# A larger landing allowance for streamed weight halves and parked value rows in a hand-planned two-layer transformer kernel

## The chip, the cores and the metric

The kernel runs on one core of one Trainium2 chip. The metric is the device time of one execution in microseconds. The kernel before takes 3228.07 us, the median of three executions (3224.22 to 3236.77 us).

## What is computed

Two layers stand one after the other twice: A, an attention with a recurrent memory, and B, a mixer and an MLP. The sequence has 2048 rows of width 640 in bf16. A works on 64 segments of 32 rows; 8 memory rows come ahead of each segment, and the first 8 rows of a segment's output are the memory of the next one, so the segments follow one another strictly. It has 32 heads of width 192.

```python
def _A_ref(x, mem0, Wq, Wk, Wv, Wo, seg_len):
    mem = mem0
    for s in range(n_seg):                      # 64 segments
        h = concat([mem, x[:, s*32:(s+1)*32, :]], axis=1)      # 40 rows x 640
        q, k, v = h @ Wq, h @ Wk, h @ Wv        # 32 heads x 192
        p = softmax(where(mask, q @ k.T * scale, -1e9))
        o = (p @ v) @ Wo
        mem = o[:, :8, :]; outs.append(o[:, 8:, :])

def _B_ref(x, w1, w2, w3, w4):
    h = gelu(layernorm(x) @ w1)
    hs = shifted_quarters(h) @ w2               # rows shifted by 1 and 2, both ways
    x1 = x + hs
    return x1 + gelu(layernorm(x1) @ w3) @ w4   # 640 -> 1536 -> 640

x = x + A(layernorm(x)); x = x + B(layernorm(x))
x = x + A(layernorm(x)); x = x + B(layernorm(x))
```

## The kernel before

**Steps and lanes.** The two passes through A run in one loop of 69 steps. In step t lane 0 does segment t of the first A and lane 1 segment t-5 of the second A (`LAG = 5`), so that steps 5 to 63 have both lanes, with 80 rows together, and the five steps at either end have one lane with 40. The B layers run beside it in chunks of 64 rows per lane, one chunk for two steps (`chunk`, `chunk_end`).

**One step.** The 32 heads are 8 groups of four, taken as four pairs. For a group TensorE makes keys and queries (`keys_queries`, L1789, tiles psk and psq, 30 matmuls of 80 columns for each), then scores (L1914, tile pss), the transposed probabilities (L1949, pst), the weighted values (L1966, pso) and the output projection (L1992, psy). Values of a pair are made at once: in an odd step for the two steps t and t+1 together (L1836), the rows of the next step being parked in DRAM (`vahead`, stored at L1844 by the POOL queue) and fetched back in the even step (L1874), in which TensorE makes only the 32 rows that were missing (L1863). The B chunk puts its matmuls (L2299, L2359, L2422, L2468) between these.

**Weights.** Wq, Wk and Wv do not all fit into SBUF. Of the five blocks of 128 input rows, `STREAM` gives for each pair how many are streamed in every step (4, 2, 2, 4 for keys and queries, 3, 1, 1, 4 for values); the others stay resident (tiles wk, wq, wv). A streamed block of a pair comes as two halves, one for each group, 128 x 768 bf16 or 192 KB each (`load_pair`, L1647, tile wst). They go into a ring of 24 slots (`RING_A`). The order of pairs is reversed in odd steps, so that the last pair of a step is the first of the next one and its halves, 22 or 24 slots, stay in the ring over the step's end. B's weights come in tiles of up to 320 KB (`load_b`, L1683 to L1689, tile wstB) through three slots. All of these loads are issued by the SP queue.

**The plan.** The program is first written as a list of operations, each with an engine, a duration, what it reads and writes, and the bytes of its DMA if it is one. `Plan.add` gives each a priority from the table `RANK`: one number for each operation of a kind of step (all even steps with both lanes share "step0", all odd ones "step1", the chunks between the ends "chunk" and "chunk_end"), in units of 1/67108864 us counted from the step's nominal start at 48 us a step. `Plan.place` sorts the operations of every engine by that number, and this sorted line is the order in which the engine's instructions are issued. It then walks through all lines with the durations and finds a planned start and end for each operation. A transfer is planned so:

```python
srv = max(s + DMA_FIRST, srv) + o.dma / (DMA_START if o.due < STEP else RATE_ONE if alone(o) else DMA_RATE)
done = srv + DMA_LAST + o.margin
```

with `DMA_FIRST = 0.8`, `DMA_LAST = 3.2` and `DMA_RATE = 315.0e3` bytes a microsecond. `done` is when the plan lets readers start. Three things follow from the planned times. The slots of a ring (and the PSUM banks) are given to operations in the order in which the plan sees them come free. A load that the plan holds back so as not to run ahead of the transfers in flight is marked `paced`, and is made to wait for the last TensorE operation that the plan has finished by then (`PACE`, at the end of the program). And the list in which instructions are written out is the plan's. The engines themselves know nothing of planned times: they run their line in order and wait for semaphores.

Loads of half blocks had no margin, B's loads have 0.6 us (`B_MARGIN`), the two `vahead` transfers had 0.7.

**Around a step's end.** The memory columns of the next step are copied from psy by VectorE (L2019). The rows of the next segment of lane 1 come from the chunk two steps before: transposes on TensorE (L2522, `ft4`) and copies into hT by ScalarE (L2530, `fc`). The first keys of a step read both.

Of the kernel before, what the change touches and what calls it, by code (L numbers as in the profile page):

```python
# [29 lines left out]
LOOK = 48  # L30
# [26 lines left out]
DMA_ISSUE = 0.37  # L57
# [21 lines left out]
        "apply_ln.f": (619821940, 1419652867, 3136865741, 3492529800,),  # L79
        "chunk.f1": (-1862542,),  # L80
        "chunk.f2": (535234527,),
        "chunk.f3": (1353287692,),
        "chunk.fe": (870238683,),
        "chunk.fe3": (3486582945,),
        "chunk.fel": (1557734022,),
        "chunk.fhr": (1765481928,),
        "chunk.fhs": (3007050626,),
        "chunk.fk0": (326638728,),
        "chunk.fk1": (2726001406,),
        "chunk.fs": (3218780102, 3249069099,),  # L90
        "chunk.ft": (240166152,),
        "chunk.ftl": (1496228237,),
        "chunk.fw": (1622229593, 1701935762, 1679143945, 3102708780, 2859414961, 2758250835, 3572172952,
            3606843237, 3536726401, 4173573343, 4121567882, 4086897597, 4513907470,),
        "chunk.fx": (280917415,),
        "chunk.fx0": (1611157029, 1591751692,),
        "chunk.fxu": (3495585980,),
# [6 lines left out]
        "load_b.fn": (-375525581, -730077448, -719610040, 2385923537, 2300994965, 2236236914, 2786142732,  # L104
            2909490384, 3152783868, 3707910948, 3558408627, 3606655073, 4125914395,),
        "transposes.f": (692464316, 3455587541,),
    },
    "chunk_0": {
        "apply_ln.f": (232141763, 341066263, 2067097874,),
        "chunk.f1": (-8505083173,),  # L110
        "chunk.f2": (-3934198857,),
        "chunk.f3": (429532210,),
        "chunk.fe": (489648082,),
        "chunk.fe3": (2067500527,),
        "chunk.fel": (489756973,),
        "chunk.fhr": (890745413,),
        "chunk.fhs": (1309035218,),
        "chunk.fk0": (947777863,),
        "chunk.fs": (1483668581, 1483869908,),
        "chunk.ft": (8946517,),  # L120
        "chunk.ftl": (632649931,),
        "chunk.fw": (771015019, 772787850, 771440545, 1256902217, 1257159630, 1256986807, 2238393962,
            2223390616, 2230674554, 2933112234, 2722326263, 2721658280, 3302745147,),
        "chunk.fx": (48195564,),
        "chunk.fx0": (732303114, 704855262,),
        "chunk.fxu": (2308563139,),
# [6 lines left out]
        "load_b.fn": (-3381292124, -3550034551, -865167426, 661737317, 901566278, 877089128, 1887363173,  # L133
            1723063724, 1770985122, 2367901289, 1963995011, 1996230009, 2750184683,),
        "transposes.f": (232343089, 1986629510,),
    },
    "chunk_1": {
        "apply_ln.f": (234352147, 424171623, 1139471209, 2036067845,),
        "chunk.f1": (-2741551,),
        "chunk.f2": (234150821,),  # L140
        "chunk.f3": (615954977,),
        "chunk.fe": (846136918,),
        "chunk.fe3": (2142881513,),
        "chunk.fel": (1047394441,),
        "chunk.fhr": (1126500078,),
        "chunk.fhs": (1691122064,),
        "chunk.fk0": (629977546,),
        "chunk.fk1": (783871166,),
        "chunk.fs": (1764784013, 1837791043,),
        "chunk.ft": (37634002,),  # L150
        "chunk.ftl": (679799131,),
        "chunk.fw": (1069660796, 1087512398, 1069363349, 1633744337, 1639274557, 1638655619, 2164198979,
            2250875979, 2143082840, 2698140225, 2881958716, 2728577128, 3229969347,),
        "chunk.fx": (77677747,),
        "chunk.fx0": (1019473581, 982935782,),
        "chunk.fxu": (2162451645,),
# [6 lines left out]
        "load_b.fn": (-579470846, -623813017, -964754743, 1067636933, 1158283287, 1183355579, 1764991342,  # L163
            1842237442, 1752739776, 2259173599, 2382650117, 2334628335, 2800447638,),
        "transposes.f": (399648704, 2036269172,),
    },
    "chunk_2": {
        "apply_ln.f": (292538731, 581557556, 1720999575, 2087329837,),
        "chunk.f1": (-1067306343,),
        "chunk.f2": (-917191276,),  # L170
        "chunk.f3": (383995904,),
        "chunk.fe": (571492627,),
        "chunk.fe3": (2206858353,),
        "chunk.fel": (574304103,),
        "chunk.fhr": (1075922126,),
        "chunk.fhs": (1728010341,),
        "chunk.fk0": (142581676,),
        "chunk.fk1": (1048460664,),
        "chunk.fs": (1730498649, 1730699975,),
        "chunk.ft": (6693347,),  # L180
        "chunk.ftl": (454388984,),
        "chunk.fw": (795548396, 873443794, 964470025, 1661674941, 1712556472, 1730190881, 2417607530,
            2407364944, 2408544805, 2859361305, 3144040297, 2867698681, 3424642378,),
        "chunk.fx": (21942750,),
        "chunk.fx0": (454590310, 464307541,),
        "chunk.fxu": (2124830409,),
# [6 lines left out]
        "load_b.fn": (-1455669518, -1022821962, -1141274702, 977129502, 914535287, 1285206154, 1774812963,  # L193
            1813367340, 1806473275, 2519856677, 2545492615, 2511697104, 2589146350,),
        "transposes.f": (292740058, 2192345064,),
    },
    "chunk_end": {
        "apply_ln.f": (6207473151,),
        "chunk_end.fc": (6407041413, 6407041413, 6932872812,),
        "chunk_end.fs": (5783564718, 5813267330,),  # L200
        "chunk_end.fst": (6203127175, 6017353691,),
        "chunk_end.ft4": (6406840087,),
        "chunk_end.fw": (5008812969, 5667704631, 5308788779, 5110805706, 5701443477, 5735182323,),
        "chunk_loads.f": (6259009269, 5903203514, 6038126415, 6070862680, 6014976291,),
        "ln_ops.f1": (5842969942,),
        "ln_ops.f2": (6164006683,),
# [1209 lines left out]
def kernel(  # L1416
# [17 lines left out]
    P = 128  # L1434
# [10 lines left out]
    GW = HG * Dh  # L1445
# [8 lines left out]
    VP = 2 * Dh + 64  # L1454
# [130 lines left out]
    add = plan.add  # L1585
# [1047 lines left out]
```

## Time and profile before

| What | Before |
|---|---|
| median of three executions | 3228.07 us (3224.22 to 3236.77) |
| the profiled execution, its own time | 3227.25 us |
| span of the profile, first to last instruction | 3225.5 us |
| mean granted TensorE clock | 0.991 |
| TensorE matmul busy | 3106.5 us |
| TensorE weight load busy | 2765.5 us |
| VectorE, ScalarE, GpSimd busy | 2052.9, 1723.4, 497.3 us |
| moved by DMA | 859.75 MB, mean 267 GB/s |

The profiled execution lies within the three others, so its times can be set beside their median. What remains between its time and its span, 1.75 us, lies outside the instructions. PE stands for TensorE's matmuls, PEld for its weight loads, DVE for VectorE, ACT for ScalarE, POOL for GpSimd, SP for the queue that issues the weight loads. An entry "X <- Y" in a list of waits says that engine X sat idle until Y released it.

### The profile page before, as it was taken

The page shows a single profiled execution, that of the slowest core. Times are in us where ns is not written, and L with a number is a line of the kernel's source. Part 1 is how long each engine was busy: PE and PEld are TensorE (multiplying, and loading weights), DVE is VectorE, ACT ScalarE, POOL GpSimd, SP SyncE. Part 2 cuts the span into 40 slices and gives each one's busy share as a digit, 9 for nine tenths or more (in the row PEclk, how much of TensorE's full clock was granted, in tenths as well). Part 3 has the DMA queues.
Part 4 walks back from the last instruction along what each step waited for, and adds up shares of the span by engine and source line. Part 5 has one row for each costly group of instructions (what it writes and reads, how often), then busy time and mean ns, then how long its engine had stood idle before and what let it go on. Part 6 is the DMA issues. An engine that isn't in the chain of part 4 may idle for free.

```text
span 3225.5 us, 161658 instructions
## 1 busy us (share of the span) xinstructions
PE 3106.5 (96%) x70199; PEld 2765.5 (86%) x70201; DVE 2052.9 (64%) x6448; ACT 1723.4 (53%) x3985; POOL 497.3 (15%) x983
## 2 busy tenths in 40 slices
PE   5889999999999999999999999999999999999898
PEld 4778889988888888888889888888888888888776
DVE  2565666666666666666666666666666666666665
ACT  1334555555555555555555555555555555556443
POOL 0001111111111111111111111111111111110000
PEclk7999999999999999999999999999999999999999
DMA  9887888888888888888888888888888888888786
GB/s 362 264 279 246 255 282 267 258 259 271 265 263 267 277 252 255 263 283 260 260 277 272 258 256 266 276 263 260 280 263 257 258 269 269 263 263 284 245 281 213
DMA packets 636978, 859.75 MB, mean 267 GB/s; under 512 B 72254, under 2 KB 622863, under 8 KB 636264
## 3 DMA queue, kind: packets, MB, share of 16 engines
q1 hardware_dynamic: 612056, 796.18, 77.5%
q0 software_dynamic: 24032, 53.12, 5.4%
q8 instruction: 550, 9.01, 1.2%
q14 instruction: 164, 1.34, 0.1%
q10 hardware_dynamic: 176, 0.09, 0.0%
HBM read 823.73 MB, written 25.37 MB: 263 GB/s over the span
## 4 chain that ended last, share of the span: by engine, by line
PE 80%; DMA 14%; issue 2%; DVE 1%; ACT 1%; POOL 0%; SPq 0%; POOLq 0%; ACTq 0%; DVEq 0%
PE psy L1992 16%; PE psk L1789 15%; PE psq L1789 15%; PE psv L1836 11%; DMA wst<-in_A_Wk_dram 6%; PE pso L1966 4%; PE pss L1914 4%; DMA wst<-in_A_Wq_dram 4%; PE psh L2422 3%; PE psv L1863 3%; PE y L2468 3%; PE pst L1949 2%; PE hs L2359 1%; PE psv L1894 1%; DMA wst<-in_A_Wv_dram 1%
## 5 line engine op out<-in xcount | busy, mean ns | idle before, releaser
L1789 PEld LDWEIGHTS <-wst 128*128 128x128 bf16 x19872 | 822.0, 99 | 127.8 <-DMA wst<-in_A_Wk_dram 31.7
L1992 PE MATMUL psy<-oT,wo 128*128 128x80 bf16 (+1 forms) x16560 | 695.9, 200 | 3.2 <-issue 1.0
L1992 PEld LDWEIGHTS <-wo 128*128 128x128 bf16 x16560 | 628.8, 99 | 27.6 <-issue 13.8
L1789 PE MATMUL psk<-hT,wst 128*128 128x80 bf16 (+1 forms) x9936 | 568.1, 200 | 37.2 <-DMA wst<-in_A_Wk_dram 23.3
L1824 ACT CAST V<-psv 128x384 bf16<-128x384 f32 (+4 forms) x1032 | 485.8, 474 | 199.1 <-PE psv L1863 75.5
L1789 PE MATMUL psq<-hT,wst 128*128 128x80 bf16 (+1 forms) x9936 | 550.0, 200 | 26.0 <-DMA wst<-in_A_Wq_dram 21.3
L1799 ACT CAST qT<-psq 128x480 bf16<-128x480 f32 (+1 forms) x552 | 291.5, 528 | 519.3 <-PE psq L1789 441.7
L1814 DVE CAST kT<-psk 64x160 bf16<-64x160 f32 (+1 forms) x1104 | 339.2, 307 | 132.6 <-PE psk L1789 87.8
L1937 DVE TENSOR_REDUCE sm<-Pm 80x4 f32<-80x320 bf16 (+2 forms) x552 | 249.9, 453 | 248.1 <-ACT Pm L1933 243.2
L1974 ACT CAST oT<-pso 128x480 bf16<-128x480 f32 (+1 forms) x552 | 293.8, 533 | 164.1 <-PE pso L1966 147.8
L1926 DVE CUSTOM_DVE_ANT_1 pss<-pss,mask 80x320 f32<-80x320 f32 (+2 forms) x552 | 258.0, 468 | 186.6 <-PE pss L1914 112.5
L1933 ACT ACTIVATE Pm<-pss,sm 80x320 bf16<-80x320 f32 (+2 forms) x552 | 279.7, 507 | 170.6 <-DVE sm L1926 107.7
L1957 ACT COPY PT<-pst 80x320 bf16<-80x320 bf16 (+2 forms) x552 | 221.3, 401 | 203.4 <-PE pst L1949 182.8
L1789 PE MATMUL psk<-hT,wk 128*128 128x80 bf16 (+1 forms) x6624 | 320.7, 200 | 2.0 <-issue 1.3
L1789 PE MATMUL psq<-hT,wq 128*128 128x80 bf16 (+1 forms) x6624 | 320.0, 200 | 2.5 <-DMA wq<-in_A_Wq_dram 1.8
L1807 DVE CAST kT<-psk 128x320 bf16<-128x320 f32 (+1 forms) x552 | 254.8, 462 | 91.3 <-PE psk L1789 57.3
L1836 PEld LDWEIGHTS <-hT 128*128 128x128 bf16 x2320 | 204.9, 98 | 101.4
L1939 DVE TENSOR_TENSOR Pm<-Pm,sm 80x320 bf16<-80x320 bf16 (+2 forms) x552 | 255.8, 463 | 44.9 <-DVE sm L1938 0.5
L1836 PE MATMUL psv<-wv,hT 128*128 128x384 bf16 x1276 | 284.1, 327 | 0.0
L1789 PEld LDWEIGHTS <-wk 128*128 128x128 bf16 x6624 | 272.1, 100 | 7.2 <-issue 3.3
L1789 PEld LDWEIGHTS <-wq 128*128 128x128 bf16 x6624 | 266.0, 99 | 4.1 <-DMA wq<-in_A_Wq_dram 1.9
L1844 POOL DMA_DIRECT2D vahead<-V x232 | 119.9, 519 | 932.7 <-ACT V L1824 921.9
(140 smaller groups left out, 4112.8 us busy)
## 6 DMA issues: line engine op xcount, KB each, us to landing
wst<-in_A_Wq_dram SPq DMA_DIRECT2D x1112, 192.0 KB, 4.6
wst<-in_A_Wk_dram SPq DMA_DIRECT2D x1112, 192.0 KB, 4.5
wstB<-in_B_w_dram SPq DMA_DIRECT2D x495, 320.0 KB, 4.8
wst<-in_A_Wv_dram SPq DMA_DIRECT2D x766, 192.0 KB, 4.7
wstB<-in_B_w_dram SPq DMA_DIRECT2D x132, 160.0 KB, 4.1
vahead<-V POOLq DMA_DIRECT2D x232, 84.0 KB, 4.3
V<-vahead POOLq DMA_DIRECT2D x232, 84.0 KB, 4.8
wo<-in_A_Wo_dram SPq DMA_DIRECT2D x8, 960.0 KB, 10.2
```

Of the source, the lines that this page charges most:

```text
L1789: nc.tensor.matmul(out=o[:, cc, 0:W], lhsT=wv(kc, GW * j + cc * P, GW * j + (cc + 1) * P), rhs=h[:, kc, cw:cw + W], start=begin(pq), stop= ...
L1799: nc.scalar.copy(out=qT[G % QT_BUFS][:, :, c0:c0 + N], in_=T(pq)[:, :, off:off + N])
L1807: nc.vector.tensor_copy(out=k4[:, :, 0::3, c0:c0 + N], in_=p4[:, :, 0::2, off:off + N])
L1814: copy(out=k4[r0:r1, :, jj, c0:c0 + N], in_=p4[r0:r1, :, 1, off:off + N])
L1824: (nc.vector.tensor_copy if e == "DVE" else nc.scalar.copy)(out=v_part(*dst), in_=a_)
L1836: nc.tensor.matmul(out=T(bank)[:], lhsT=left[:, kc, :], rhs=wv(kc, GWH * b, GWH * (b + 1)), start=(kc == 0), stop=(kc == KC - 1))
L1926: nc.vector.tensor_tensor_reduce(out=o, in0=o, in1=maskt.unsqueeze(1).to_broadcast([NR, HG, N]), scale=-scale, scalar=3.0e38, op0=ALU.add, ...
L1933: nc.scalar.activation(out=Pb[0:NR, :, 0:N], in_=o, func=ACT.Exp, bias=sm_[0:NR, 0:1], scale=-1.0)
L1937: nc.vector.tensor_reduce(out=sm_[0:NR, 2:2 + HG], in_=Pb[0:NR, :, 0:N], axis=AX.X, op=ALU.add)
L1939: nc.vector.tensor_tensor(out=Pb[0:NR, :, 0:N], in0=Pb[0:NR, :, 0:N], in1=sm_[0:NR, 6:6 + HG].unsqueeze(2).to_broadcast([NR, HG, N]), op=A ...
L1974: nc.scalar.copy(out=o_[:, :, off:off + N], in_=T(pso)[:, :, 0:N])
L1992: nc.tensor.matmul(out=o[:, m, cw:cw + W], lhsT=wo[:, cc, m * P:(m + 1) * P], rhs=o_[:, cc, 0:W], start=st, stop=True, skip_group_check=True)
```

## The change

Three `margin` arguments change: loads of half blocks get 0.8 us where they had none, and the two `vahead` transfers 1.2 us instead of 0.7. Nearly every number of `RANK` is replaced (4871 of 4880); the table's keys, and the count of numbers under each, stay. No operation is added or removed, and no tile, size, buffer count or constant of the plan differs otherwise.

```diff
-            add("SP", DMA_ISSUE, due - now + 0.005 * u, fn, w=(b,), dma=2 * P * GW, queue="wa")
+            add("SP", DMA_ISSUE, due - now + 0.005 * u, fn, w=(b,), dma=2 * P * GW, queue="wa",
+                margin=0.8)
...
                     add("POOL", 0.6, s0 + 0.3, fst, r=(B("V", j, 0, 0), B("V", j, 1, 0), B("V", j, "s")),
-                        w=(B("vahead", pr, j),), dma=LOOK * 2 * VP * 2, margin=0.7)
+                        w=(B("vahead", pr, j),), dma=LOOK * 2 * VP * 2, margin=1.2)
...
                     add("POOL", 0.6, s0 - 2.0 + j * sl, fst, r=(B("vahead", pr, j),), w=(B("V", j, "s"),),
-                        dma=LOOK * 2 * VP * 2, margin=0.7)
+                        dma=LOOK * 2 * VP * 2, margin=1.2)
```

Of the table, the rows that are spoken of below; in "load_pair.fn" stand the loads of halves, in "attention_step.keys_queries.fn" the groups of matmuls that read them:

```diff
     "chunk_end": {
-        "chunk_end.fc": (6407041413, 6407041413, 6932872812,),
-        "chunk_end.ft4": (6406840087,),
+        "chunk_end.fc": (6382708409, 6391570887, 6408253138,),
+        "chunk_end.ft4": (6359822874,),
...
     "step0": {
...
-            1046104218, 1331991171, 1166383760, 1841544131, 1852522656, 1508134442, 1747519327, 1549091689,
...
-            -26594931, 771222703, 369935051, 618351194, 531851907, 62865026, 822179872, 317650874, 946387944,
...
+            1004419520, 1033225886, 819629740, 871488755, 987133137, 1363609596, 1346323213, 1502503537,
...
+            545383571, 71783088, 1293155743, 1170835110, 1070473733, 1716573390, 896663422, 1443704250,
...
     "step1": {
...
-            2181380150, 2332687929, 2301536345, 2368998866, 2259032793, 2258661668, 2470491963, 2386401162,),
...
-            1908463971, 831762713, 2076412523, 2298565453, 2259808074, 1792191834, 1400585187, 2221050695,
...
+            756957187, 680740191, 477165011, 743507109, 783857343, 581793785, 770407265, 918462051,
...
+        "load_pair.fn": (83574525, 317849987, -80935802, 44528614, 200712256, 161666345, 278804077, 536669669,
```

More of the change, by code (lines that the diff above doesn't have):

```diff
@@ L106 @@
-        "transposes.f": (692464316, 3455587541,),
+        "apply_ln.f": (528439666, 1281802442, 2772655964, 3378771941,),
+        "chunk.f1": (-1876410,),
+        "chunk.f2": (454069850,),
+        "chunk.f3": (1314767112,),
+        "chunk.fe": (860163803,),
+        "chunk.fe3": (3467028034,),
+        "chunk.fel": (1545788341,),
+        "chunk.fhr": (1788466643,),
+        "chunk.fhs": (2676300140,),
+        "chunk.fk0": (1001201985,),
+        "chunk.fk1": (2232885900,),
+        "chunk.fs": (3135065722, 3218817387,),
@@ L107 @@
+        "transposes.f": (797184262, 3419901535,),
     },
     "chunk_0": {
[L109 to L119, printed above, removed]
@@ L135 @@
-        "transposes.f": (232343089, 1986629510,),
+        "apply_ln.f": (251361110, 362569255, 1918297637,),
+        "chunk.f1": (-3389571368,),
+        "chunk.f2": (-3336291060,),
+        "chunk.f3": (432776927,),
+        "chunk.fe": (366081486,),
+        "chunk.fe3": (1999486533,),
+        "chunk.fel": (702804528,),
+        "chunk.fhr": (842860529,),
+        "chunk.fhs": (1884021852,),
+        "chunk.fk0": (887245114,),
+        "chunk.fs": (1629427860, 1664812252,),
+        "chunk.ft": (19883116,),
@@ L136 @@
+        "transposes.f": (329158381, 1962557389,),
     },
     "chunk_1": {
[L138 to L148, printed above, removed]
@@ L165 @@
-        "transposes.f": (399648704, 2036269172,),
+        "apply_ln.f": (417078095, 884102030, 1701955989, 2054078969,),
+        "chunk.f1": (-166472186,),
+        "chunk.f2": (-31756890,),
+        "chunk.f3": (626432597,),
+        "chunk.fe": (676651504,),
+        "chunk.fe3": (2151820299,),
+        "chunk.fel": (730827102,),
+        "chunk.fhr": (1014004451,),
+        "chunk.fhs": (1582458834,),
+        "chunk.fk0": (167355508,),
+        "chunk.fk1": (884303357,),
+        "chunk.fs": (1860971164, 1861172491,),
@@ L166 @@
+        "transposes.f": (587615776, 2113001063,),
     },
     "chunk_2": {
[L168 to L178, printed above, removed]
@@ L195 @@
-        "transposes.f": (292740058, 2192345064,),
+        "apply_ln.f": (300151518, 380441880, 1600227838, 2060102732,),
+        "chunk.f1": (-1304639093,),
+        "chunk.f2": (-21342998,),
+        "chunk.f3": (409318233,),
+        "chunk.fe": (488493588,),
+        "chunk.fe3": (2120940987,),
+        "chunk.fel": (569957715,),
+        "chunk.fhr": (1068366767,),
+        "chunk.fhs": (2007668140,),
+        "chunk.fk0": (295221622,),
+        "chunk.fk1": (1110624813,),
+        "chunk.fs": (1939879576, 1940080903,),
@@ L220 @@
+        "chunk_end.ft4": (6625126752,),
+        "chunk_end.fw": (3623643191, 3795896206, 4373039738, 5473903407, 4606760246, 5704572181,),
+        "chunk_loads.f": (6114147133, 6195519747, 5773587820,),
+        "ln_ops.f1": (6026447153,),
+        "ln_ops.f2": (6276892361,),
+        "load_b.fn": (2782658394, 2656932143, 3638961977, 4944262055, 3982461976, 5184712042,),
     },
     "chunk_end_1": {
-        "apply_ln.f": (5001053806,),
-        "chunk_end.fc": (5552113032, 5601463238, 5560887287,),
@@ new lines @@
+        "chunk_end.fc": (5560788764, 5742476953, 5505128029,),
+        "chunk_end.fs": (4803334859, 4836965648,),
+        "chunk_end.fst": (5554344322,),
+        "chunk_end.ft4": (5365217002,),
+        "chunk_end.fw": (3633410563, 3823121637, 4645611500, 4048108251, 4749667731, 4557022991,),
+        "chunk_loads.f": (5046367897, 4938796327, 6036306674, 4875518944, 4803335866,),
+        "ln_ops.f1": (4870596436,),
+        "ln_ops.f2": (5002073709,),
+        "load_b.fn": (2735053028, 2918661439, 4035746013, 3587773333, 4328295357, 3918724585,),
@@ L242 @@
[L242 to L243 removed]
+        "apply_ln.f": (6147793798,),
+        "chunk_end.fc": (6378022691, 7479015835, 7415357164,),
+        "chunk_end.fs": (5578266745, 5815410512,),
+        "chunk_end.fst": (5913127144, 5852407581,),
+        "chunk_end.ft4": (6353340871,),
+        "chunk_end.fw": (3771302616, 4071017304, 4788464869, 5145454449, 5296541945, 4445354989,),
+        "chunk_loads.f": (6203789660, 6034172717, 6143070097, 6264509223, 5348042013,),
@@ L269 @@
+        "chunk_end.fst": (6170200328, 6579369759,),
+        "chunk_end.ft4": (6409147219,),
+        "chunk_end.fw": (4689269515, 4614206962, 4765603287, 5887478322, 5980223003, 5948953378,),
+        "chunk_loads.f": (6446780128, 6513074944,),
+        "chunk_loads.fz": (6353203130,),
+        "ln_ops.f1": (5980424329,),
+        "ln_ops.f2": (6293466440,),
+        "load_b.fn": (4042538175, 3790370482, 4186633980, 5249340829, 5429460552, 5339400690,),
     },
     "chunk_end_tail2": {
-        "apply_ln.f": (5693383719,),
@@ new lines @@
+        "chunk_end.fc": (6214857121,),
+        "chunk_end.fs": (5745344525, 5789279728,),
+        "chunk_end.fst": (5931494050, 6099580590,),
+        "chunk_end.ft4": (6153464515,),
+        "chunk_end.fw": (4020543645, 3927927498, 4619715811, 5664579394, 4871999210, 5551077718,),
+        "chunk_loads.f": (10006497999, 6182246070,),
+        "chunk_loads.fz": (5839643524,),
+        "ln_ops.f1": (5864597238,),
+        "ln_ops.f2": (6014159530,),
+        "load_b.fn": (2839327835, 2769364924, 4018708192, 5135368272, 3931468825, 4943441612,),
@@ L804 @@
-        "start.f2": (-64227062230,),
-        "start.f3": (-64226860904,),
-        "start.f4": (-64227464884,),
-        "start.f5": (-64226860904, 91931784, 2703611270, 6716436040,),
-        "transposes.f": (-64227062230,),
+        "apply_ln.f": (-670688907,),
+        "chunk_loads.f": (3158728332, 3126543583, 269593842,),
+        "ln_ops.f1": (-670890234,),
+        "ln_ops.f2": (-670688907,),
+        "start.f1": (-1940671501,),
+        "start.f2": (-1940470175,),
+        "start.f3": (-1940268848,),
```

1516 lines of the change are left out of this document (722 added, 794 removed), and 463 rows, old and new, of the table RANK.

## The prediction

> **What bounds the kernel now.** I read the page's first part and the chain of waits, then the busy time by stage, then what TensorE waited for in each stage.
>
> ```profile
> span 3225.5 us, 161658 instructions
> PE 3106.5 (96%) x70199; PEld 2765.5 (86%) x70201; DVE 2052.9 (64%) x6448; ACT 1723.4 (53%) x3985; POOL 497.3 (15%) x983
> PE 80%; DMA 14%; issue 2%; DVE 1%; ACT 1%; POOL 0%; SPq 0%; POOLq 0%; ACTq 0%; DVEq 0%
> ```
>
> TensorE is the bound: no other engine is busy for two thirds of the span, and 80% of the chain is its own work. The rest of the chain is nearly all DMA, 14%. So the time can fall by at most what TensorE sits idle, 3225.5 - 3106.5 = 119 us, less what it must wait for anyway. By stage:
>
> ```profile
> core 0: us, PE busy (x) PEld busy (x) DVE busy (x) ACT busy (x) POOL busy (x), PEclk, DMA share, GB/s
> 0.00:50.00 50.00, 23.97 (x418) 19.95 (x418) 12.30 (x45) 6.15 (x16) 7.33 (x30) 0.77 1.00 359
> 50.00:250.00 200.00, 169.51 (x4442) 141.29 (x4444) 112.33 (x421) 72.62 (x219) 10.06 (x20) 0.94 0.87 286
> 250.00:2950.00 2700.00, 2667.29 (x59194) 2399.22 (x59192) 1762.63 (x5406) 1527.73 (x3435) 461.06 (x896) 1.00 0.84 265
> 2950.00:3226.00 276.00, 245.72 (x6157) 205.06 (x6151) 165.63 (x577) 116.90 (x317) 18.86 (x37) 0.99 0.78 253
> ```
>
> The idle time is 26.0 us in the first 50 us, 30.5 in the one-lane steps after them, 32.7 in the 2700 us with two lanes, and 30.3 at the end. The DMA engines are 84% busy at 265 GB/s in the long stage and moved 359 GB/s in the first 50 us: there a transfer is late, not the total of them. What TensorE waited for in the second, third and fourth stage:
>
> ```profile
> PE psq L1789 <- DMA wst<-in_A_Wq_dram: 8.3, 11, 4.5
> PE psk L1789 <- DMA wst<-in_A_Wk_dram: 4.3, 5, 2.1
> ...
> PE psk L1789 <- DMA wst<-in_A_Wk_dram: 10.9, 22, 1.5
> PE psk L1789 <- ACT hT L2530: 7.2, 28, 0.3
> PE psq L1789 <- DMA wst<-in_A_Wq_dram: 3.5, 9, 0.6
> PE pso L1966 <- DMA V<-vahead: 3.2, 5, 1.3
> ...
> PE psq L1789 <- DMA wst<-in_A_Wq_dram: 6.1, 7, 2.1
> PE psk L1789 <- DMA wst<-in_A_Wk_dram: 1.9, 4, 0.6
> ```
>
> (Total, times, longest.) Halves that had not landed cost 12.6 us in 16 waits in the early steps, 14.4 us in 31 waits with two lanes, 8.0 us in 11 waits at the end; parked value rows cost 3.2 us in 5 waits. They are all that the changed margins speak of: 38.2 us. In the first 50 us the loads of two steps' weights fill the DMA engines (share 1.00), and no plan shortens that; I leave it out.
>
> Why they are late is in the landing times:
>
> ```profile
> wst<-in_A_Wq_dram SPq DMA_DIRECT2D x1112, 192.0 KB, 4.6
> wst<-in_A_Wk_dram SPq DMA_DIRECT2D x1112, 192.0 KB, 4.5
> V<-vahead POOLq DMA_DIRECT2D x232, 84.0 KB, 4.8
> DMA to landing us min/median/max: 2.3/4.6/10.8
> ```
>
> The last row is that of the halves' line. By the plan's formula a half that finds the queue empty lands 0.8 + 196608/315000 + 3.2 = 4.62 us after its issue, which is the median measured. About half of the halves are thus later than the plan has them, whenever it puts a reader right behind. In the chain, two of the waits look like this:
>
> ```profile
> 1054.02 0.03 PE pss L1914
> 1054.05 6.05 DMA wst<-in_A_Wk_dram
> 1060.11 0.05 issue
> ...
> 1065.73 0.22 PE pss L1914 x6
> 1065.95 6.43 DMA wst<-in_A_Wk_dram
> 1072.38 0.05 issue
> ```
>
> A paced load starts as TensorE ends the scores that it was made to wait for, and lands 6.05 and 6.43 us later: 1.4 and 1.8 over the plan.
>
> **The change, part by part.** No instruction is added or removed, so the busy 3106.5 us stay; only order, slots and paces move.
>
> First, *the order*. The engines obey the table's order, so the margins act only if the table has them in. It has: I took, in the numbers of the diff, the distance from each streamed half's load to the first group of matmuls that reads it, for the three pairs that a two-lane step loads (32 halves of keys and queries). The shortest was (1331991171 - 946387944) / 67108864 = 5.75 in "step0" and becomes (987133137 - 545383571) / 67108864 = 6.58; in "step1" it goes from (2386401162 - 2076412523) / 67108864 = 4.62 to (918462051 - 536669669) / 67108864 = 5.69. The one-lane steps at the end show more: in "tail3" six of 32 stand under 5.0 and the shortest at 2.68, afterwards none under 7.06. (These units are stretched to 48 a step, so they order, and aren't microseconds of the chip.) The closest readers get about 0.8 more room.
>
> What this is worth: a wait shorter than 0.8 goes, a longer one loses 0.8. With two lanes 31 waits hold 14.4 us, 0.46 on average, and the longest is 1.5; I take 12 of 14.4. For the value rows, with 0.5 more room and a longest of 1.3, 2 of 3.2. Early, 16 waits with longest of 4.5 and 2.1 keep at least 3.7 + 1.3 = 5.0 of 12.6; I take 6 off. At the end the longest of 2.1 keeps 1.3 of 8.0; I take 5 off. Sum 25 us; the bounds are 0 and 38.2.
>
> Second, *the step's start*. "chunk_end.ft4" moves from 6406840087 to 6359822874, that is 0.70 earlier, and the three copies behind it from 95.47, 95.47 and 103.31 to 95.11, 95.24 and 95.49 (divided as above; the step that reads them starts at 96). Today the first keys of every second step wait for such a copy, 7.2 us in 28 times, 0.26 each. The copies move by 0.36 and 0.23, about that size. I take 3 of 7.2; the bounds are 0 and 7.2.
>
> Third, *slots and paces*. The plan's TensorE now stands still where a half is planned late, so a paced load finds an earlier matmul to wait for. Behind such a load on SP stand all other weight loads; the row that prices these waits is
>
> ```profile
> SPq L1647 <- PE psk L1789: 474.2, 511, 12.7
> SPq L1647 <- PE psq L1789: 170.8, 325, 2.6
> ```
>
> for the two-lane stage, and they are hidden as long as the half lands before its reader, as all but 31 of its readers show. I price it with the first part and not again.
>
> Fourth, *what is paid for the room*. Every load that must stand further ahead of its reader needs its slot earlier. Over a step's end the ring holds 22 or 24 halves of 24 for the next step's first pair, so the next pair's loads wait for that step's first matmuls, and what TensorE does until they land (resident blocks, the kept pair, projections) has to stretch by as much as the margin. The two tables show the filling: in "step0" 18 groups of keys and queries stood ahead of the first scores, now 20. Where there is nothing to fill with, the half is waited for as today. The trace doesn't show the new order, so I bound: nothing if the filling is free; if it is dear, 0.8 us at each of the 58 step ends between
>
> ```profile
> L2019 DVE CAST hT<-psy x58: 240/242/244, 305.4 to 2944.1; 128x80 bf16<-128x80 f32 x58
> ```
>
> or 46 us. Moving work to cover one end tends to open a small bubble elsewhere, of the size of the present 0.26: I take 28 x 0.26 = 7.3 us.
>
> Sum: 3227.3 - 25 - 3 + 7.3 = 3206.6 for an execution like the profiled one, which stands 0.8 under the median; so 3207.4, told as 3207.
>
> The Trainium skill, "DMA: Bandwidth & Descriptors", section "Queues, rings and completion order", says that each DMA engine takes turns between the queues that have work, a packet at a time. By that a half is late because POOL's or another queue's packets came between, and a fixed 0.8 would not follow how many did. The trace has such a second queue (5.4% of the engines' time against 77.5%) and a longest landing of 10.8, so the rule isn't against it; no row ties a late half to it.
>
> **The rivals.**
>
> *The waits stay.* Late halves come in bursts: the longest landing is 10.8 us against a median of 4.6, and a TensorE that no longer waits at one place arrives earlier at the next. Then the margin takes off few, some 5 us in all, and the moved order gives 3 back: 3226. For it speaks that the largest waits (4.5, 2.1, 2.1) are far above 0.8; against it, that with two lanes 0.46 is the mean. The rule just cited would give this too.
>
> *The ring's turn becomes the bound (slower).* Place: the loads that follow a step's end. If the filling that the plan found is work whose own inputs (scores, probabilities, copies) are late on the chip, TensorE waits there in every step. At half of the bound, 0.4 us x 58, it costs 23; with the same 28 us won, 3222; with the halves still late, 3227 + 23 = 3250; at the full price 3274. It decides from about 0.75 us a step end against my gains, or from 0.28 (16 us) if the waits stay. For it speaks that both tables differ in every place, and that only 32.7 of 2700 us are idle today, so a new order has much to lose and little to win; against it, that in the new tables the distances within a group are hardly shorter: in "step1" the least from "attend.f3" (normalised probabilities) to "attend.f4" (their transposes), taken like those above, goes from 1.19 to 1.94.
>
> *All of it goes.* If the new order also removes the remaining waits with two lanes and the ends' stalls (38.2 + 7.2, and some 5 of the small waits on other engines), with nothing paid, 3228 - 50 = 3178. Only the row sums speak for it.
>
> **How the numbers follow.** The forecast gets 0.42, the waits that stay 0.24, the ring's turn 0.24, all of it 0.10. A measurement of this kernel can tell about 0.5% from no change: 16 us, under 3212 or over 3244. The forecast's own range, 25 us won with 6 more or 10 less and 0 to 12 paid, is 3196 to 3220; 0.34 of its 0.42 lie under 3212. With the last case faster has 0.44. The waits that stay put 0.22 within and 0.02 above, the ring 0.03 within and 0.21 above: same 0.33, slower 0.23. The range is 3186 to 3250: it leaves out part of the case in which all goes, and the ring's turn beyond half price.
>
> **What would show it.** Right: the waits of L1789 for halves fall from 14.4 to about 2 us with two lanes, from 12.6 to about 7 before and 8.0 to 3 behind; the rows of L2530 and of V<-vahead shrink; TensorE's busy time stays within a few microseconds of 3106.5; the first and last memory copies (L2019) stand some 10 us closer together than 305.4 and 2944.1. Wrong: the waits fall and others of TensorE, for ScalarE, VectorE or with no cause shown, rise by as much; or the waits for halves stay; or busy time itself moves, since I hold it fixed: more switches between forms of matmul, or a lower clock than 0.991.

## The result and the profile after

Twenty executions of each kernel gave a median of 3214.97 us (3209.60 to 3225.16) for the changed one and 3224.34 us (3216.17 to 3236.78) for the one before: 9.4 us less, a ratio of 0.9973 with a 95% interval of 0.9961 to 0.9985. The change makes the kernel faster, by less than half of the 21 us forecast, and within the 0.5% that the prediction called "the same". (The forecast started from 3228.07, the median of three executions; twenty put the kernel before 3.7 us lower.)

The first part of the changed kernel's page and its chain of waits:

```profile
span 3216.6 us, 161608 instructions
PE 3105.1 (97%) x70199; PEld 2762.6 (86%) x70201; DVE 2067.6 (64%) x6448; ACT 1724.2 (54%) x3985; POOL 495.0 (15%) x983
PE 87%; DMA 9%; issue 2%; DVE 1%; ACT 1%; POOL 0%; SPq 0%; ACTq 0%; POOLq 0%; DVEq 0%
```

TensorE is busy for the same time (3106.5 before), so what was won was idle time, and the chain has 9% of DMA where it had 14%. (Lines of the code stand three lower than before: L1786 is the old L1789.) What TensorE waited for with two lanes (250 to 2950 us), the rows on transfers and on the copies at a step's start:

```profile
PE psk L1786 <- ACT hT L2527: 6.9, 27, 0.3
PE psq L1786 <- DMA wst<-in_A_Wq_dram: 2.8, 8, 0.6
PE pso L1963 <- DMA V<-vahead: 2.0, 2, 1.6
PE psh L2419 <- DMA wstB<-in_B_w_dram: 1.4, 3, 0.8
...
PE psk L1786 <- DMA wst<-in_A_Wk_dram: 1.1, 4, 0.5
PE y L2465 <- DMA wstB<-in_B_w_dram: 1.0, 3, 0.5
...
PE psq L1786 <- ACT hT L2527: 0.3, 1, 0.3
```

Halves of keys and queries: 14.4 us in 31 waits before, 3.9 in 12 now. Parked value rows: 3.2 to 2.0. The copies: 7.2 before, and 6.9 + 0.3 now, since one of the waits has moved from keys to queries: nothing. The waits for B's tiles, whose margin didn't change, are 2.4, from 0.2. The same view for the early one-lane steps (50 to 250 us), all rows on transfers but one of 0.2 us:

```profile
PE psk L1786 <- DMA wk<-in_A_Wk_dram: 6.7, 1, 6.7
...
PE psq L1786 <- DMA wq<-in_A_Wq_dram: 2.2, 1, 2.2
...
PE hs L2356 <- DMA wstB<-in_B_w_dram: 1.8, 2, 1.3
PE psk L1786 <- DMA wst<-in_A_Wk_dram: 1.6, 2, 1.2
PE psq L1786 <- DMA wst<-in_A_Wq_dram: 1.6, 2, 0.9
...
PE psv L1891 <- DMA wst<-in_A_Wv_dram: 1.4, 1, 1.4
PE psh L2419 <- DMA wstB<-in_B_w_dram: 1.4, 1, 1.4
```

The keys' and queries' halves fell from 12.6 to 3.2 us as asked. But now resident blocks (wk, wq) and B's tiles are late: these rows together come to 16.7 us. Before, it was the halves' 12.6 and these rows of the same view, 15.3 in all:

```profile
PE psh L2422 <- DMA wstB<-in_B_w_dram: 1.6, 1, 1.6
...
PE psy L1992 <- DMA wo<-in_A_Wo_dram: 0.6, 1, 0.6
...
PE y L2468 <- DMA wstB<-in_B_w_dram: 0.5, 1, 0.5
```

At the end (from 2950 us on) the halves cost 4.1 us for 8.0:

```profile
PE psk L1786 <- DMA wst<-in_A_Wk_dram: 2.9, 7, 1.0
...
PE psq L1786 <- DMA wst<-in_A_Wq_dram: 1.2, 2, 0.9
```

The memory copy at a step's end marks the stages: the first of the two-lane copies ends the early part, the last of them begins the end.

```profile
L2016 DVE CAST hT<-psy x58: 240/242/243, 309.6 to 2941.2; 128x80 bf16<-128x80 f32 x58
```

| Stage, profiled executions | Before | Changed |
|---|---|---|
| start to first two-lane copy | 305.4 | 309.6 |
| 57 two-lane steps | 2638.7 | 2631.6 |
| last two-lane copy to the end of the span | 281.4 | 275.4 |

These are single executions, and executions of one program spread by 20 us, so which of the three differences are the change's had to be asked of more kernels.

### The profile page after: what moved, and what is told of

Read it like the earlier page. It is cut to its first block, busy times and chain, and to the rows that moved or that the text cites. A ratio compares the mean times of both kernels' runs of the same rounds, so it can differ in the third digit from the quotient of the medians.

```text
span 3216.6 us, 161608 instructions
## 1 busy us (share of the span) xinstructions
PE 3105.1 (97%) x70199; PEld 2762.6 (86%) x70201; DVE 2067.6 (64%) x6448; ACT 1724.2 (54%) x3985; POOL 495.0 (15%) x983
## 4 chain that ended last, share of the span: by engine, by line
PE 87%; DMA 9%; issue 2%; DVE 1%; ACT 1%; POOL 0%; SPq 0%; ACTq 0%; POOLq 0%; DVEq 0%
PE psy L1989 17%; PE psk L1786 16%; PE psq L1786 16%; PE psv L1833 11%; PE pso L1963 4%; PE pss L1911 4%; PE psh L2419 3%; PE psv L1860 3%; PE y L2465 3%; DMA wst<-in_A_Wk_dram 3%; PE pst L1946 2%; DMA wst<-in_A_Wq_dram 2%; DMA wstB<-in_B_w_dram 2%; PE psv L1891 2%; PE hs L2356 1%
## 5 line engine op out<-in xcount | busy, mean ns | idle before, releaser
L1786 PEld LDWEIGHTS <-wst 128*128 128x128 bf16 x19872 | 821.3, 99 | 83.5 <-issue 17.6
L1821 ACT CAST V<-psv 32x384 bf16<-32x384 f32 (+3 forms) x1032 | 486.1, 472 | 297.6 <-PE psv L1833 204.3
L1786 PE MATMUL psq<-hT,wst 128*128 128x80 bf16 (+1 forms) x9936 | 554.4, 200 | 16.5 <-DMA wst<-in_A_Wq_dram 12.2
L1786 PE MATMUL psk<-hT,wst 128*128 128x80 bf16 (+1 forms) x9936 | 541.4, 200 | 19.1 <-DMA wst<-in_A_Wk_dram 8.2
L1930 ACT ACTIVATE Pm<-pss,sm 80x320 bf16<-80x320 f32 (+2 forms) x552 | 278.0, 504 | 164.7 <-PE pst L1946 84.3
L1786 PE MATMUL psk<-hT,wk 128*128 128x80 bf16 (+1 forms) x6624 | 315.7, 200 | 10.7 <-DMA wk<-in_A_Wk_dram 10.3
L1786 PE MATMUL psq<-hT,wq 128*128 128x80 bf16 (+1 forms) x6624 | 316.0, 200 | 4.3 <-DMA wq<-in_A_Wq_dram 2.2
L1786 PEld LDWEIGHTS <-wk 128*128 128x128 bf16 x6624 | 266.1, 99 | 16.4 <-DMA wk<-in_A_Wk_dram 10.7
L1786 PEld LDWEIGHTS <-wq 128*128 128x128 bf16 x6624 | 266.8, 100 | 6.4 <-issue 3.1
## 6 DMA issues: line engine op xcount, KB each, us to landing
wo<-in_A_Wo_dram SPq DMA_DIRECT2D x8, 960.0 KB, 11.1
```

Source lines behind the costliest of these rows:

```text
L1786: nc.tensor.matmul(out=o[:, cc, 0:W], lhsT=wv(kc, GW * j + cc * P, GW * j + (cc + 1) * P), rhs=h[:, kc, cw:cw + W], start=begin(pq), stop= ...
L1821: (nc.vector.tensor_copy if e == "DVE" else nc.scalar.copy)(out=v_part(*dst), in_=a_)
L1930: nc.scalar.activation(out=Pb[0:NR, :, 0:N], in_=o, func=ACT.Exp, bias=sm_[0:NR, 0:1], scale=-1.0)
```

## The experiments

"Halves" (those of values among them) and "value rows" in this table are what TensorE waited for them between 310 and 2940 us, "two-lane" the time between the marks above, both in the profiled execution; the ratio is that of the executions of a kernel to those of the kernel before on the same chip, with its 95% interval. A profiled execution can lie some microseconds from the median of its kernel (the second 3210.36 for 3217.37, the ninth 3204.05 for 3210.62), so that a single two-lane time says little.

| Kernel | halves, us | value rows, us | two-lane, us | ratio |
|---|---|---|---|---|
| before | 14.2 | 3.2 | 2638.7 | 1 |
| changed | 3.9 | 2.0 | 2631.6 | 0.9973 (0.9961 to 0.9985) |
| 1 margins only | 10.9 | 7.5 | 2637.9 | 0.9996 (0.9980 to 1.0012) |
| 2 table only | 3.2 | 1.4 | 2627.1 | 0.9982 (0.9968 to 0.9997) |
| 3 start of before | 4.0 | 2.0 | 2629.8 | 0.9970 (0.9958 to 0.9982) |
| 4 new in the middle only | 5.5 | 1.0 | 2630.2 | 0.9988 (0.9974 to 1.0001) |
| 5 new at the ends only | 14.9 | 3.2 | 2641.0 | 0.9990 (0.9977 to 1.0003) |
| 6 before, issued earlier | 3.1 | 4.6 | 2629.7 | 0.9962 (0.9948 to 0.9977) |
| 9 changed, issued earlier | 0 | 2.1 | 2622.7 | 0.9974 (0.9964 to 0.9984) |
| 10 before, earlier still | 3.5 | 10.9 | 2634.5 | 0.9994 (0.9981 to 1.0008) |
| 11 before, earlier everywhere | 4.4 | 3.6 | 2625.5 | 0.9968 (0.9953 to 0.9982) |
| 12 combined | 1.7 | 1.5 | 2629.1 | 0.9968 (0.9952 to 0.9985) |

**1 and 2: is it the margins or the table?** The kernel before with the margins alone:

```diff
-            add("SP", DMA_ISSUE, due - now + 0.005 * u, fn, w=(b,), dma=2 * P * GW, queue="wa")
+            add("SP", DMA_ISSUE, due - now + 0.005 * u, fn, w=(b,), dma=2 * P * GW, queue="wa",
+                margin=0.8)
...
-                        w=(B("vahead", pr, j),), dma=LOOK * 2 * VP * 2, margin=0.7)
+                        w=(B("vahead", pr, j),), dma=LOOK * 2 * VP * 2, margin=1.2)
...
-                        dma=LOOK * 2 * VP * 2, margin=0.7)
+                        dma=LOOK * 2 * VP * 2, margin=1.2)
```

> The kernel before with the three new margins and its own table: every engine keeps its order, only slots, paces and the written order follow the stretched plan. Theory (the table's order carries the gain): TensorE still arrives at the same halves in the same order, the waits for halves with two lanes stay above 8 of 14.4 us, ratio to before 0.999 to 1.001. Rival (slots and paces carry it: paced loads are hung on earlier matmuls): waits for halves fall to about 4 us as in the changed kernel, ratio about 0.997.

Its waits with two lanes:

```profile
PE pso L1967 <- DMA V<-vahead: 7.5, 8, 2.3
PE psk L1790 <- ACT hT L2531: 7.2, 28, 0.3
PE psk L1790 <- DMA wst<-in_A_Wk_dram: 6.9, 15, 1.5
PE psq L1790 <- DMA wst<-in_A_Wq_dram: 3.0, 6, 1.2
```

Slots and paces alone take 3.3 us off the halves and put 4.3 on the value rows; the ratio is 1 within its interval. The opposite, the new table with the margins of before:

```diff
-                margin=0.8)
+                margin=0.0)
...
-                        w=(B("vahead", pr, j),), dma=LOOK * 2 * VP * 2, margin=1.2)
+                        w=(B("vahead", pr, j),), dma=LOOK * 2 * VP * 2, margin=0.7)
...
-                        dma=LOOK * 2 * VP * 2, margin=1.2)
+                        dma=LOOK * 2 * VP * 2, margin=0.7)
```

> The new table with the old margins (0 and 0.7): the changed order, with paces and slots of a plan that trusts the shorter landing. Theory (order): ratio to before 0.997, as the whole change, waits for halves with two lanes about 4 us. Rival (slots and paces): ratio 0.999 to 1.001, waits for halves back above 8 us.

```profile
PE psq L1786 <- DMA wst<-in_A_Wq_dram: 1.5, 5, 0.6
PE pso L1963 <- DMA V<-vahead: 1.4, 2, 1.1
PE psk L1786 <- DMA wst<-in_A_Wk_dram: 1.2, 4, 0.4
```

The waits are as short as in the whole change, the two-lane stage is 12 us shorter than before, and the ratio's interval lies below 1 and overlaps that of the change. So the order carries the gain, and with it in place nothing is seen that the margins add. That rests on the waits and the stage: the ratios' intervals of the first and second kernels overlap.

**3, 4 and 5: in which stage?** The third kernel is the changed one with the table's "start", "first" and "second" of before.

```diff
+RANK["start"], RANK["first"], RANK["second"] = (the rows of before)
...
-                margin=0.8)
+                margin=(0.0 if due < 2 * STEP else 0.8))
```

> The changed kernel, but the table's rows for the program's start and the first two steps are those of before, and the halves of these two steps have no margin. Theory (the new table's start costs some 6.5 us, 97.6 against 91.1 us to the first memory copy, since resident blocks come late and the loads stand behind slots of values): the first memory copy is back at about 91 us and the ratio to before is 0.995. Rival (that difference is chance between two executions): first copy anywhere from 91 to 98, ratio 0.997.

The first memory copy came at 94.4 us, the ratio is 0.9970: my reading of the two profiles was wrong. With the table's start of before the copy came at 91.1 (before), 92.4 (1), 92.9 (4), 94.4 (3), 96.3 (6) and 95.4 us (10); with the new one at 97.6 (changed), 94.7 (2), 94.8 (5) and 94.1 us (9). The two groups overlap, and the 6.5 us between the first two profiles were mostly chance.

The fourth (upper part, made from the changed kernel, with its margins) has the new rows only from step 6 to step 61, the fifth (lower part, made from the one before, with the margins of before) only outside (start to step 6, and from step 64 on). The rows are put in short here.

```diff
+RANK["start" to "head5", "chunk_0", "chunk_1", "chunk_end_0", "chunk_end_1", all "tail", "end", "last"] = (the rows of before)
...
+RANK["start" to "head6", "chunk_0" to "chunk_2", "chunk_end_0" to "chunk_end_2", "tail2" on, "end", "last"] = (the new rows)
```

> The changed kernel with the table's rows of before for the start, steps 0 to 5 with their chunks, and everything from step 62 on; the new order holds in between. Theory (the two-lane stage has 7 us of the gain, the end 6, the start loses 6.5): first to last two-lane memory copy about 2632 us as in the changed kernel, ratio 0.998. Rival (the two-lane stage's 7 us are chance and the ends carry all): 2638 us there, ratio 1.000.

> The kernel before, with its margins, and the new table's rows at both ends only: the start and steps 0 to 6 with their chunks, and from step 64 on. The complement of the fourth run. Theory as it stands after the first four runs (all of the gain lies in the two-lane stage): first to last two-lane memory copy 2638 us, ratio to before 0.999 to 1.002. Rival (the waits for halves that the ends lost, 12.6 to 3.2 and 8.0 to 4.1 us, are a gain there as predicted, some 10 us): ratio 0.997.

The two nearly complement each other (step 6 is new in both, steps 62 and 63 in neither). The two-lane stage took 2630.2 us where its order is new and 2641.0 where it isn't; the marks:

```profile
L1519 DVE CAST hT<-psy x58: 240/241/243, 305.7 to 2935.9; 128x80 bf16<-128x80 f32 x58
```

```profile
L1518 DVE CAST hT<-psy x58: 240/242/243, 307.1 to 2948.1; 128x80 bf16<-128x80 f32 x58
```

Over all kernels whose two-lane order and issue are those of before (before, 1, 5) the stage takes 2639.2 us on average, with the new order (changed, 2, 3, 4) 2629.7: 9.5 us less. (The seventh and eighth below, whose two-lane steps are those of the changed kernel, took 2625.6 and 2627.8.) At the ends nothing is left. To the first two-lane copy the old table took 305.4, 299.1, 305.7, 307.9 and 304.9 us (before, 1, 4, 6, 10), 304.6 on average, the new one 309.6, 303.2, 307.1 and 304.9 (changed, 2, 5, 9), 306.2. Counted from the first memory copy, whose own time varies, it is 211.0 and 210.9. From the last copy on the old one took 281.4, 278.6, 276.3, 274.6 and 279.1 (same kernels), 278.0, the new one 275.4, 278.4, 278.5, 280.6 and 274.8 (changed, 2, 3, 5, 9), 277.5. The total of the fourth kernel, 0.9988, is short of what its middle would give, but its interval holds 0.9974, and the fifth's excludes the 0.997 of the rival.

**6, 9 and 10: will any room do?** The sixth kernel is the one before with one constant changed. A paced load may then be issued 1.65 us ahead of the planned transfers in flight, and keeps its place in every queue.

```diff
-DMA_AHEAD = 0.85
+DMA_AHEAD = 1.65
```

> The kernel before with its own table and margins, but paced loads may be issued 0.8 us earlier against the planned transfers (DMA_AHEAD 1.65 for 0.85). Theory (a half is late because its reader stands a median landing behind its issue; any 0.8 us of room will do): waits for halves with two lanes fall from 14.4 to about 4 us, ratio 0.996 to 0.998. Rival (the slot, not the pace, sets when a load can go, so only another order of TensorE's work makes room): waits stay above 8 us, ratio 0.999 to 1.001.

```profile
PE psk L1789 <- ACT hT L2530: 7.2, 28, 0.3
PE pso L1966 <- DMA V<-vahead: 4.6, 7, 1.3
...
PE psk L1789 <- DMA wst<-in_A_Wk_dram: 1.6, 6, 0.4
PE psq L1789 <- DMA wst<-in_A_Wq_dram: 1.5, 3, 0.7
```

The halves' waits fall from 14.2 to 3.1 us, the stage from 2638.7 to 2629.7, and the ratio, 0.9962, is no worse than that of the whole change. It was the room, not the place where it was found: leave to issue loads 0.8 us earlier does what 4871 new numbers do.

The ninth puts both together (the same line in the changed kernel); the tenth doubles the step in the kernel before (`DMA_AHEAD = 2.45`).

> The changed kernel, and paced loads with two lanes may go 0.8 us earlier (DMA_AHEAD 1.65). Theory (the two are the same room won twice; only some 4 us of waits for halves and 2 us for value rows are left with two lanes): ratio to before 0.995 to 0.9975, no clear step beyond the change alone. Rival (the new order pays something for its room, and with earlier issue the halves land earlier still, so that both add): ratio 0.993 or less.

> The kernel before with DMA_AHEAD 2.45: the sixth run's step taken twice, table and margins of before. Theory (0.8 us covers nearly all late halves, 14.4 to about 3 us, so a second step finds nothing): ratio to before as in the sixth run, 0.9955 to 0.997. Rival (with more loads in flight each lands later after its issue, and takes the slots and the value rows' transfers with it): median landing of a half above 5 us and ratio 0.998 or more.

Together no wait for a half is left with two lanes and the stage is the shortest of all, 2622.7 us, but in a profiled execution 6.6 us under the median, and the total, 0.9974, isn't told apart from the change alone. Doubled, the gain is gone:

```profile
PE pso L1966 <- DMA V<-vahead: 10.9, 12, 1.8
...
PE psk L1789 <- DMA wst<-in_A_Wk_dram: 2.2, 7, 0.5
...
PE psq L1789 <- DMA wst<-in_A_Wq_dram: 1.3, 2, 0.7
```

The halves are on time, but the value rows, which POOL fetches, are late instead: 10.9 us for 3.2. The transfers' own rows of the tenth kernel (310 to 2930 us) show them landing later:

```profile
wst<-in_A_Wk_dram SPq DMA_DIRECT2D x909, 192.0 KB, 4.8
wst<-in_A_Wq_dram SPq DMA_DIRECT2D x906, 192.0 KB, 4.8
...
V<-vahead POOLq DMA_DIRECT2D x230, 84.0 KB, 5.1
```

These medians rose by 0.2 to 0.3 us (4.5, 4.6 and 4.8 before in the same stretch). The theory that a second step finds nothing to do was wrong in kind: it takes something away. The expected landing above 5 us was wrong too: with halves landing after 4.8 the value rows are late already. These account for 6.3 of the some 10 us between the ratios of the sixth kernel and this one (10.9 for 4.6); where the rest was lost isn't shown. The Trainium skill, "DMA: Bandwidth & Descriptors", section "Issuing engines are not separate DMA queues", says that transfers of all issuing engines run on the same 16 DMA engines and interleave; these rows agree.

**7, 8 and 11: what holds the ends?** In the seventh kernel the halves asked for in steps 1 to 4 and from step 64 on bring an eighth of their rows.

```diff
+        light = STEP <= due < LAG * STEP or due >= NSTEPS * STEP
...
-                nc.sync.dma_start(out=T(b)[:], in_=w_src[kind][:, kc, c0:c0 + GW])
+                rows = P // 8 if light else P
+                nc.sync.dma_start(out=T(b)[0:rows, :], in_=w_src[kind][0:rows, kc, c0:c0 + GW])
...
-            if kc < nres:
-                return rt[:, kc, c0:c1]
+            if kc < nres or light:
+                return rt[:, kc % nres, c0:c1]
```

> The changed kernel, but the halves asked for in steps 1 to 4 and from step 64 on fetch only 16 of their 128 rows, and their matmuls read a resident block instead; the same instructions, order, slots and paces, and an eighth of these bytes (the result leaves those blocks' weights out). Theory (in the one-lane steps the chain within a step sets the pace as much as the landing does, so taking waits for halves away there moves the wait to another engine): the one-lane steps stay at 39 to 41 us where they were 37 to 43. Rival (they are bound by the bytes: a step moves some 11 MB): they fall to 35 us or less.

It took 3182.86 us (one execution). Windows of 150 us in the early steps, the changed kernel and then this one:

```profile
100.00:250.00 150.00, 133.76 (x3721) 113.91 (x3716) 93.70 (x354) 58.05 (x176) 8.30 (x17) 0.99 0.85 271
```

```profile
100.00:250.00 150.00, 143.06 (x3997) 122.93 (x3994) 101.97 (x383) 65.62 (x199) 8.30 (x17) 1.00 0.38 100
```

(PE, PEld, DVE, ACT, POOL, clock, share of the DMA engines' time, GB/s.) The DMA engines' share falls from 0.85 to 0.38, TensorE's idle time from 16.2 to 6.9 us, and 276 more matmuls fit in. The part up to the first two-lane copy is 17.2 us shorter (292.4 for 309.6), the end 12.2 (3181.2 - 2918.0 = 263.2 for 275.4). The four early one-lane steps take 35.3, 38.3, 37.7 and 38.3 us for 36.6, 42.4, 40.9 and 43.3, 3.4 less each; together 149.6, where the other kernels' profiles have 157.9 to 164.9, so one execution is enough here. So the theory as I wrote it (39 to 41) falls: what the one-lane steps lose beside TensorE's own work, they lose in good part to transfers. From the first memory copy to the first two-lane one TensorE's waits for transfers fall from 8.9 us to this one row:

```profile
PE hs L2358 <- DMA wstB<-in_B_w_dram: 0.6, 1, 0.6
```

The rival's 35 us aren't reached either, and the trace shows what holds the rest: TensorE is busy for 143.06 of 150 us, by which a mean step of 37.4 us has about 35.7 of its own work (an estimate from this row).

The eighth and eleventh loosen the brake on the loads there: how far one may run ahead of the planned transfers, and how many may be in flight.

```diff
-DMA_AHEAD_ONE = 1.0
+DMA_AHEAD_ONE = 3.0
...
-FLYING = 9
+FLYING = 14
```

> The changed kernel with the brake on loads in the one-lane steps loosened: up to 3 us ahead of the planned transfers instead of 1, and 14 loads in flight instead of 9. Theory (the chain within a step): steps unchanged within 1 us each. Rival (the brake holds loads back): the one-lane steps get shorter by 1 us or more each; if the transfers are what is scarce, halves only land later after their issue (above the 4.6 us median) and nothing is won.

> The kernel before with its table and margins, DMA_AHEAD 1.65 with two lanes, and at the ends 3 us ahead for 1 and 14 loads in flight for 9. Theory (the one-lane steps are held by their transfers, and a brake that is loosened starts them earlier): one-lane steps about 1 us shorter each, ratio 0.994 to 0.996. Rival (there the transfers are as dense as they can be, 85 to 88% busy with the slots full, and the eighth run's 3210 us was chance): ratio as in the sixth run, 0.996 to 0.997.

The eighth (the changed kernel, one execution) took 3209.86 us, its early one-lane steps 36.6, 43.3, 41.0 and 40.1: three within 1 us of the changed kernel's, the fourth 3.2 shorter, so neither theory holds as written, and since the kernels' fourth steps vary from 39.9 to 44.1 us nothing follows from it. The eleventh (the kernel before, with the sixth's edit too) has 0.9968 against 0.9962 of the sixth: nothing that can be measured was won by the brake.

**12: all that seemed to help, together**: the third kernel with the lines of the sixth and the eighth.

> The changed kernel with the table's start and first two steps of before (third run), DMA_AHEAD 1.65 with two lanes (ninth run), and at the ends 3 us ahead and 14 loads in flight (eighth and eleventh runs). Theory (room in the two-lane stage, some 12 us, is one gain however it is won, and the loosened brake adds some 3 to 5 us at the ends): ratio to before 0.9955 to 0.997. Rival (the gains add: change 9 us, start 2, earlier issue 3, ends 5): 0.994.

With 0.9968 it is at the theory's upper end and not better than any of its parts. No kernel here is shown to beat the changed one beyond the intervals; the sixth does as well with one line.

## Why the prediction was right in kind and wrong in size

**The order's distances** were the right thing to read from the diff: the table alone gives the short waits and the short stage (2), the margins alone don't (1), as far as two overlapping intervals and the traces tell.

**Halves with two lanes**: "I take 12 of 14.4"; 10.5 went (14.4 to 3.9). **Value rows**: 2 of 3.2; 1.2 went. Over the kernels with the old two-lane order (before, 1, 5) and the new one (changed, 2, 3, 4) the averages of the table fall by 9.2 and 3.0. **What is paid for the room**: 7.3. By these averages the waits fell by 12.2 us and the stage by 9.5, so that 2.7 were paid. For what isn't shown: B's tiles, whose rows went from 0.2 to 2.4 us in the first two profiles, cost 2.9 in the fifth kernel, which has the old order there. That too much room costs something showed in kernel 10, where POOL's transfers paid for SP's.

**The step's start**: 3 of 7.2; nothing went. The copies did move ahead, but so did their readers: in the tables the first group of keys in "step0" moves from -17592500 to -44623634, that is 0.40 earlier, as much as the copies (0.36 and 0.23). I compared the copies with the step's nominal start instead of with the instruction that waits. The traces show why no rank of the copies helps: before,

```profile
1045.03 0.31 PE L2522 MATMUL psn<-ident,h2u 128*128 128x64 bf16 x5
...
1045.38 0.36 ACT L2530 CAST hT<-psn 128x10 bf16<-128x10 f32 x2 [1.74 <-PE psn L2522]
...
1045.60 0.38 PE L1789 MATMUL psk<-hT,wst 128*128 128x80 bf16 x6 [0.26 <-ACT hT L2530]
```

and in the changed kernel

```profile
1049.31 0.31 PE L2519 MATMUL psn<-ident,h2u 128*128 128x64 bf16 x5
...
1049.66 0.55 ACT L2527 CAST hT<-psn 128x10 bf16<-128x10 f32 x3 [1.74 <-PE psn L2519]
...
1049.88 0.38 PE L1786 MATMUL psk<-hT,wst 128*128 128x80 bf16 x6 [0.26 <-ACT hT L2527]
```

In both the transposes are the last that TensorE does ahead of the first keys, at all 29 such step ends, and it has nothing to do while ScalarE copies. Other work of TensorE between the two would be needed; no run tried that.

Together the two-lane stage was forecast at -12 - 2 - 3 + 7.3 = -9.7 us, and the kernels of the experiments differ by 9.5 (-9.2 - 3.0 + 2.7): right by luck in part, since the gains were taken 4.8 too large and the price 4.6 too large.

**The ends** are where the step failed: "I take 6 off" early and "I take 5 off" at the end, 11 us of which the kernels show -1.6 and 0.5. I took a wait of TensorE for a half as time that comes back when the half is on time. With two lanes most of it did: 9.5 of 12.2 us. In the one-lane steps the halves' waits fell in the two profiles (12.6 to 3.2, and 8.0 to 4.1 at the end), and on average over the kernels the stages didn't get shorter. Part of that fall is chance: among the kernels with the old table there (before, 1, 4, 6, 10) the waits for halves go from 3.6 to 11.1 us between the first memory copy and the first two-lane one, and from 3.5 to 8.2 behind the last two-lane one. On average they are 6.7 and 5.9 us with the old table and 4.0 and 4.3 with the new one (the kernels averaged above). But TensorE's waits for all transfers together, with resident blocks and B's tiles, are 8.2 and 6.3 us with the old and 8.0 and 6.1 with the new: what a half no longer holds up, another transfer does. That fewer bytes do shorten these steps is shown by kernel 7. Without these two terms the sum is 3227.3 - 17 + 7.3 = 3217.6, or 3218 with the 0.8 up to the median; from the median of twenty, 3224.3 - 9.7 = 3214.6, where 3215.0 was measured.

**The rivals.** That the waits stay, with 3226, fell for the two-lane stage: a fixed 0.8 us took most of the waiting for halves away (14.2 to 3.1 us in 6). Whether packets of other queues had come between isn't shown. The ring's turn as the bound fell too: the two-lane stage got shorter. That all of it goes, with 3178, fell by the waits that are left. But the first had the right reason for the ends: a TensorE that no longer waits at one place waits at the next.

## What to carry to other kernels

Before a wait for a transfer is counted as a gain, add up the waits for all transfers of that stage, in more than one kernel that shares it: at the ends here the sum stayed and the wait only changed its name. The DMA engines' share of time didn't tell the stages apart (kernel before: 0.84 from 100 to 250 us, 0.85 from 310 to 2920, 0.83 from 2950 to 3180). TensorE's own did: in the same windows it was busy 89, 99 and 92% of the time, and where it was busy nearly throughout, most of a removed wait came back. Room in a plan can come from the readers' order or from earlier issue, and the cheaper one, a single constant, should be tried first; too much of it makes the transfers of other queues late. And two profiles of kernels that differ by 0.3% do not show in which stage they differ: several variants that share a stage do.

## What had not been expected of the hardware

With leave to issue loads 1.6 us earlier (10), the DMA engines' share and rate in the two-lane stage stayed (0.85 and 266 GB/s in both), and yet the median landing of halves rose from 4.5 and 4.6 us to 4.8 and that of the value rows from 4.8 to 5.1. Of the kernel only that leave was changed.

The program's start varies by itself: the same order of instructions in the first two steps (before, 1, 3, 4, 6 and 10) reached the first memory copy after 91.1 to 96.3 us, with TensorE's granted clock at 0.77 over the first 50 us of the execution before.
